# Attention with whole-row loads and one head per TensorE tile, and values @ first matrix as eight tiles, in an attention and two-layer expert kernel

## The chip, the cores and the metric

The kernel runs on one core of one Trainium2 chip. The metric is the time of the program on the device, in microseconds (us), as the median of several executions. TensorE (PE in the profile) multiplies matrices out of SBUF into the banks of PSUM; VectorE (DVE), ScalarE (ACT) and GpSimd (POOL) do elementwise work; SyncE (SP) issues all loads and stores of this kernel, and 16 DMA engines carry them.

## What is computed

Queries, keys and values have 4 batches, 8 heads, 576 rows and 64 columns, and each head has 32 packed rows p. The packed rows attend to the keys and values; then the queries attend to that packed result:

```python
p_packed = sm_attn(p, k, v)               # 32 rows a head
out = sm_attn(q, p_packed, p_packed)      # 576 rows a head
```

`sm_attn` is softmax(scale * Q K^T) V. The result, 2304 tokens by 512 columns, goes through two layers:

```python
h = x @ w_in                              # 512 -> 2048
x = (h * clip(h + 3, 0, 6) / 6) @ w_out   # 2048 -> 512
P = exp(x @ w_gate - max); 8 times: rows, then columns of P normalised
out += P[:, e:e+1] * (relu(x @ w1[e]) @ w2[e])   # for 8 experts, 512 -> 1024 -> 512
```

The two matrices of the first layer come in as 64-bit floats and are taken apart into 32-bit ones on the chip.

## The kernel before, in words

Every large product is made of three passes over operands that are split into a high and a low part (`split_part`, L417 and L422). Small products, those of the attention among them, run on plain float32 operands; such a matmul shows as two passes (two instructions) in the profile.

**Attention** (`attention`, L464) works in eight units of four heads: unit u is batch u // 2 and half u % 2 of its heads. For a unit SP issues four loads of k (L480), p (L489, in the first two units), four loads of q (L497) and one of v (L505). Keys of two heads lie side by side in one tile, so a load of one head writes runs of 64 numbers, 256 bytes, with a gap between them; q likewise. v comes in rows of 6 x 64 numbers, 1,536 bytes. There is one buffer each for k (one per pair of heads), q and v. Then, in this order of dependence:

- 12 transposes of k (L527), three to a bank, each of 96 rows by two heads, and four copies to kT (L293 on ScalarE or L294 on VectorE; this helper makes all copies out of PSUM);
- a transpose of p (L544), and a multiplication with a mask (L549), so that a head's columns stand beside zeros;
- scores of the first attention (L569): four matmuls, 128 rows deep, two heads in 64 columns of TensorE, 288 wide, into two banks; maximum, exponential, sum;
- nine transposes of q (L617), and three copies;
- six transposes of the weights (L637), two copies, and 12 matmuls with v (L653), 96 deep, 64 columns, 128 wide;
- the division, masked (L664, ppz), two transposes (L678) and two copies to ppT, a tile per unit in which each head's packed values stand beside zeros;
- the second scores in two parts, of 384 and 192 columns (L710): 18 matmuls, 128 deep, 64 columns, 64 wide; softmax over each 32 columns; transposes (L768, L772); and copies to a2 in high and low parts.

**First layer.** The result of the second attention is not formed. Instead `packed_weights` (L800) multiplies ppT of a batch's two units with 256 columns of w_in: four matmuls (L810), 128 deep, 64 columns of TensorE, 256 wide, into one bank, eight passes in all. One copy (L825, ScalarE) and one subtraction (L830, VectorE) of 512 columns make the high and low parts pw. `layer1a` (L835) multiplies a2 with pw (L848 to L850), four products of six passes for each of two halves of a batch's rows; ScalarE (L858) and VectorE (L863) apply the activation and with that free the bank. `layer2a` (L870) multiplies with w_out (L885 to L887). The group of `packed_weights` occurs 32 times: four batches by eight groups of 256 hidden units.

The banks of PSUM are shared out by tag: four of `tp` during the attention, and two each of `ph` (pw, layer1a) and `po` (layer2a), which become four each after it (`second_phase`). The group's result and each product of layer1a take one place of `ph`.

**Weights.** `whole` (L386) loads a matrix of a group: for w_in two pieces (`raw_piece`, L375; one DMA each at L381, of 128 partitions by two rows of 2,048 bytes), which `split_f64` takes apart. It has two places, `raw`. The first four groups' weights are loaded during the attention; those of the first two go ahead of unit 0.

**Order.** A planner (`Order`) puts all operations in the order in which each engine takes them: it always picks the operation that can start first by a model of the costs, and among those the most urgent. The costs are written beside each operation. Each engine, SP too, then takes its operations strictly in that order. The routing (L1067 for its product, L1077, L1137) and the eight experts (`layer1b`, L958 to L960; `layer2b`, L1007 to L1009) follow, from about 390 us on.

## Time and profile before

| | |
|---|---|
| three executions | 1982.13, 1979.96, 1975.92 us; median 1979.96 |
| the profiled execution | span 1972.3 us, first to last instruction; no other time of it is given |
| busy, share of the span | TensorE 97%, VectorE 71%, GpSimd 53%, ScalarE 44% |
| granted TensorE clock, mean over the span | 0.996 of full speed |
| DMA | 104.95 MB in 103,553 packets, of which 42,736 are under 512 bytes |
| chain of work that ended last | 71% TensorE's; its largest lines are L1007 to L1009 and L958 to L960 |

The span is that of one execution taken by the profiler. Busy time counts a matmul from its start to its modelled end, and matmuls overlap, so distances between starts are the better measure of what one costs. A group's row gives busy time, mean duration of one and the idle time of its engine just before it, with what ended that. A line of a helper (L293, L417, L422) stands for many operations, so the tile's name matters.

### The profile page before, as it was taken

The page shows a single profiled execution, that of the slowest core. Times are in us where ns is not written, and L with a number is a line of the kernel's source. Part 1 is how long each engine was busy: PE and PEld are TensorE (multiplying, and loading weights), DVE is VectorE, ACT ScalarE, POOL GpSimd, SP SyncE. Part 2 cuts the span into 40 slices and gives each one's busy share as a digit, 9 for nine tenths or more (in the row PEclk, how much of TensorE's full clock was granted, in tenths as well). Part 3 has the DMA queues.
Part 4 walks back from the last instruction along what each step waited for, and adds up shares of the span by engine and source line. Part 5 has one row for each costly group of instructions (what it writes and reads, how often), then busy time and mean ns, then how long its engine had stood idle before and what let it go on. Part 6 is the DMA issues. An engine that isn't in the chain of part 4 may idle for free.

```text
span 1972.3 us, 29636 instructions
## 1 busy us (share of the span) xinstructions
PE 1922.3 (97%) x10957; PEld 1733.2 (88%) x10957; DVE 1392.9 (71%) x2499; ACT 874.1 (44%) x1992; POOL 1052.1 (53%) x1045
## 2 busy tenths in 40 slices
PE   6999999998999999999999999999999999999998
PEld 4789989997888999999889899999999999999997
DVE  6885686437988777777866767667676676767665
ACT  6885775435354444444453334333333333333332
POOL 2454575326787766677744445454454544545442
PEclk9999999999999999999999999999999999999999
DMA  9921121001212221222301111110111111111102
GB/s 212 199 78 33 54 65 44 12 1 32 65 57 67 70 74 66 65 66 74 88 31 43 33 33 34 32 44 33 33 33 33 43 33 33 33 33 43 33 11 65
DMA packets 103553, 104.95 MB, mean 53 GB/s; under 512 B 42736, under 2 KB 78576, under 8 KB 103408
## 3 DMA queue, kind: packets, MB, share of 16 engines
q1 hardware_dynamic: 103408, 103.06, 19.0%
q8 instruction: 86, 1.41, 0.3%
q14 instruction: 59, 0.48, 0.1%
HBM read 98.32 MB, written 4.72 MB: 52 GB/s over the span
## 4 chain that ended last, share of the span: by engine, by line
PE 71%; DVE 4%; issue 1%; ACT 0%; ACTq 0%; DVEq 0%
PE po L1009 13%; PE po L1007 13%; PE po L1008 13%; PE ph L958 11%; PE ph L960 11%; PE ph L959 11%; DVE acc L1025 1%; DVE acc L1019 1%; DVE tmp L936 1%; DVE tmp L967 1%; DVE acc L1031 0%; DVE hsl L422 0%; DVE xyl L422 0%; DVE w1xl L422 0%; ACT tmp L973 0%
## 5 line engine op out<-in xcount | busy, mean ns | idle before, releaser
L422 POOL TENSOR_TENSOR hsl<-tmp,hsh 128x384 fp32r<-128x384 f32 (+1 forms) x503 | 505.1, 1019 | 541.0 <-ACT hsh L417 538.4
L1031 DVE SCALAR_TENSOR_TENSOR acc<-po,Pr,acc 128x512 f32<-128x512 f32 x504 | 373.6, 748 | 186.2 <-PE po L1009 184.8
L967 DVE TENSOR_TENSOR tmp<-ph,tmp 128x384 f32<-128x384 f32 x672 | 364.1, 554 | 165.9 <-PE ph L960 150.3
L1009 PE MATMUL po<-w2h,hsl 128*128 128x512 f32 x1152 | 449.1, 390 | 2.8 <-DVE hsl L422 2.8
L1007 PE MATMUL po<-w2h,hsh 128*128 128x512 f32 x1152 | 449.0, 390 | 1.3 <-ACT hsh L417 1.3
L1008 PE MATMUL po<-w2l,hsh 128*128 128x512 f32 x1152 | 448.8, 390 | 0.0
L973 ACT ACTIVATE tmp<-tmp 128x384 f32<-128x384 f32 x384 | 198.7, 521 | 460.1 <-DVE tmp L967 457.6
L958 PE MATMUL ph<-xyh,w1h 128*128 128x384 f32 x768 | 259.8, 338 | 7.9 <-DVE tmp L967 5.9
L959 PE MATMUL ph<-xyl,w1h 128*128 128x384 f32 x768 | 259.1, 337 | 2.3 <-DVE xyl L422 2.2
L1009 PEld LDWEIGHTS po<-w2h,hsl 128*128 128x128 f32 x1152 | 216.2, 188 | 49.8 <-DVE hsl L422 4.5
L960 PE MATMUL ph<-xyh,w1l 128*128 128x384 f32 x768 | 259.0, 337 | 0.0
L417 ACT ACTIVATE hsh<-tmp 128x384 fp32r<-128x384 f32 (+1 forms) x512 | 245.9, 498 | 22.4 <-DVE tmp L863 10.4
L1007 PEld LDWEIGHTS po<-w2h,hsh 128*128 128x128 f32 x1152 | 216.3, 188 | 43.1 <-ACT hsh L417 1.8
L1008 PEld LDWEIGHTS po<-w2l,hsh 128*128 128x128 f32 x1152 | 216.3, 188 | 41.5
L417 ACT ACTIVATE w2h<-raw 128x1024 fp32r<-128x1024 f32 x64 | 67.9, 1060 | 403.3 <-PE po L1009 394.1
L422 POOL TENSOR_TENSOR w2l<-raw,w2h 128x1024 fp32r<-128x1024 f32 x60 | 145.0, 2416 | 113.6 <-ACT w2h L417 113.6
L958 PE MATMUL ph<-xyh,w1xh 128*128 128x384 f32 x576 | 194.9, 338 | 0.5 <-ACT xyh L417 0.5
L959 PE MATMUL ph<-xyl,w1xh 128*128 128x384 f32 x576 | 194.6, 338 | 0.0
L960 PE MATMUL ph<-xyh,w1xl 128*128 128x384 f32 x576 | 194.4, 338 | 0.0
L958 PEld LDWEIGHTS ph<-xyh,w1h 128*128 128x128 f32 x768 | 144.9, 189 | 14.2 <-DVE tmp L967 4.2
L959 PEld LDWEIGHTS ph<-xyl,w1h 128*128 128x128 f32 x768 | 144.9, 189 | 6.4 <-DVE xyl L422 2.5
L960 PEld LDWEIGHTS ph<-xyh,w1l 128*128 128x128 f32 x768 | 145.0, 189 | 0.0
(186 smaller groups left out, 3242.1 us busy)
## 6 DMA issues: line engine op xcount, KB each, us to landing
raw<-in_moe_w_dram SPq DMA_DIRECT2D x128, 512.0 KB, 3.6
raw<-in_moe_w_in_dram SPq DMA_DIRECT2D x16, 512.0 KB, 3.9
raw<-in_moe_w_out_dram SPq DMA_DIRECT2D x16, 512.0 KB, 3.8
k<-in_k_dram SPq DMA_DIRECT2D x32, 144.0 KB, 5.5
q<-in_q_dram SPq DMA_DIRECT2D x32, 144.0 KB, 4.7
v<-in_v_dram SPq DMA_DIRECT2D x8, 576.0 KB, 6.7
out_dram<-acc SPq DMA_DIRECT2D x36, 128.0 KB, 2.4
p<-in_p_dram SPq DMA_DIRECT2D x1, 224.0 KB, 5.5
```

Source lines behind the costliest of these rows:

```text
L417: t_act(n), lambda: nc.scalar.activation(dst(w.t[0]), src(), AF.Copy),
L422: lambda e: e.tensor_tensor(dst(w.t[1]), src(), as_f32(dst(w.t[0])), ALU.subtract),
L936: lambda e, s=s, i0=i0, i1=i1, how=how: e.tensor_tensor(s.t, i0(), i1(), how),
L958: nc.tensor.matmul(out, wh[:, at + c, :], bh[:, c, :], start=(c == 0), stop=False)
L959: nc.tensor.matmul(out, wh[:, at + c, :], bl[:, c, :], start=False, stop=False)
L960: nc.tensor.matmul(out, wl[:, at + c, :], bh[:, c, :], start=False, stop=(c == 1))
L967: t_dve(n), lambda: nc.vector.tensor_tensor(dst.t, ps.t[:, :n], u.t, ALU.add),
L973: act(t_act(n), lambda: nc.scalar.activation(c.t, c.t, AF.Relu), writes=[c], **quick)
L1007: nc.tensor.matmul(ps.t, hh[:, f, ts], wh[:, f, :], start=(f == 0), stop=False)
L1008: nc.tensor.matmul(ps.t, hh[:, f, ts], wl[:, f, :], start=False, stop=False)
L1009: nc.tensor.matmul(ps.t, hl[:, f, ts], wh[:, f, :], start=False, stop=(f == NFC - 1))
L1031: lambda row=row, share=share, ps=ps: nc.vector.scalar_tensor_tensor(row(), ps.t, share(), row(), ALU.mult, ALU.add),
```

## The change

In the attention, keys are loaded two heads at a time, each head's six rows of a partition as one run of 1,536 bytes, and queries likewise with nine rows, 2,304 bytes: two loads of k and two of q for four of each. The transposes of k and q take two neighbouring rows of one head in place of one row of two heads, so even rows of a head land in the first 64 partitions and odd rows in the other 64. Products then take one head at a time: 64 deep, in TensorE tiles of 64 rows by 32 columns (first scores) or 64 by 64 (second scores, now with 256 and 320 columns), and 96 by 32 for the product with v. Masks, and the memsets that made them, are gone. The transposed packed rows (pt, ppT) hold the same values in both halves of the partitions, in place of values beside zeros.

In the first layer, a group of `packed_weights` is eight matmuls, 64 deep and 32 columns, on eight different tiles of TensorE, for the two units in two banks, with a copy and a subtraction of 256 columns for each bank. w_in is loaded for that in halves of 64 partitions: two DMAs for each piece.

The rest of the diff takes out comments.

```diff
     def raw_piece(src, prio, tag="raw"):
...
+    def raw_halves(srcs, prio, tag="raw"):
+        c, n = srcs[0].shape[1], srcs[0].shape[2]
+        r = hold(tag, [128, c * n], srcs[0].dtype)
+        for h, src in enumerate(srcs):
+            dma(
+                256,
+                lambda h=h, src=src: nc.sync.dma_start(
+                    r.t[64 * h:64 * h + 64].rearrange("p (c n) -> p c n", c=c), src
+                ),
+                fills=[r], prio=prio,
+            )
+        return r
...
         if which == "w1":
-            src = w1[:, f0:f0 + FG].rearrange("(c p) f -> p c f", p=128)
+            halves = [
+                w1[DM // 2 * h:DM // 2 * (h + 1), f0:f0 + FG].rearrange("(c d) f -> d c f", d=D) for h in range(2)
+            ]
+            shape, wide = [128, KC, FG], w1.dtype == I64
+            piece = lambda i, n, tag: raw_halves([s[:, i:i + n, :] for s in halves], prio, tag)
...
-        kp = [tile_of(f"k{g}", [PR, R, 2, D]) for g in range(2)]
+        kp = [tile_of(f"k{g}", [PR, 2, R, D]) for g in range(2)]
...
-        for h in range(4):
+        for g in range(2):
             dma(
                 288,
-                lambda h=h: nc.sync.dma_start(
-                    kp[h // 2].t[:, :, h % 2, :], k[b, 4 * j + h].rearrange("(p r) d -> p r d", r=R)
+                lambda g=g: nc.sync.dma_start(
+                    kp[g].t.rearrange("p h r d -> p h (r d)"),
+                    k[b, 4 * j + 2 * g:4 * j + 2 * g + 2].rearrange("h (p r) d -> p h (r d)", r=R),
                 ),
-                fills=[kp[h // 2]], **kw,
+                writes=[kp[g]], **kw,
             )
...
-                for g in range(2):
+                for h in range(4):
                     nc.tensor.matmul(
-                        s1[a].t[64 * g:64 * g + 64, :HS],
-                        pt.t[:, g, :],
-                        kT.t[:, g, a * HS:(a + 1) * HS],
+                        s1[a].t[32 * h:32 * h + 32, :HS],
+                        pt.t[64 * a:64 * a + 64, 32 * h:32 * h + 32],
+                        kT.t[64 * a:64 * a + 64, 3 * h:3 * h + 3, :].rearrange("p m c -> p (m c)"),
                         start=True, stop=True,
                     )
...
-            for r in range(R):
-                for g in range(2):
+            for n in range(R):
+                a, i = divmod(n, 3)
+                for h in range(4):
                     nc.tensor.matmul(
-                        pp.t[64 * g:64 * g + 64, :128],
-                        a1T.t[:, r, 64 * g:64 * g + 64],
-                        v_sb.t[:, 2 * g:2 * g + 2, r, :],
-                        start=(r == 0), stop=(r == R - 1),
+                        pp.t[32 * h:32 * h + 32, :D],
+                        a1T.t[:, n, 32 * h:32 * h + 32],
+                        v_sb.t[:, h, 2 * i + a, :],
+                        start=(n == 0), stop=(n == R - 1),
                     )
...
+                for h in range(4):
+                    g, o = divmod(h, 2)
+                    for r in range(4):
+                        w, c = r % 2, 128 * (r // 2) + 32 * h
+                        nc.tensor.matmul(
+                            s2.t[64 * w:64 * w + 64, c:c + 32],
+                            qT.t[lo:hi, o, r, 64 * g:64 * g + 64],
+                            ppT.t[lo:hi, 32 * h:32 * h + 32],
+                            start=True, stop=True,
+                        )
...
-        ps, w = psum("ph"), pair("pw", [128, 2, FG])
+        ps, w = [psum("ph") for _ in range(2)], pair("pw", [128, 2, FG])
 
         def mm():
-            for j in range(2):
-                for g in range(2):
+            for c in range(4):
+                for j in range(2):
                     nc.tensor.matmul(
-                        ps.t[64 * g:64 * g + 64, j * FG:(j + 1) * FG],
-                        ppTs[2 * b + j].t[:, g, :],
-                        w1.t[:, 2 * j + g, :],
+                        ps[j].t[32 * c:32 * c + 32, :FG],
+                        ppTs[2 * b + j].t[64 * j:64 * j + 64, 32 * c:32 * c + 32],
+                        w1.t[64 * j:64 * j + 64, c, :],
                         start=True, stop=True,
                     )
...
-                1.0, mm, reads=[ppTs[2 * b], ppTs[2 * b + 1], w1], writes=[ps], takes=[w],
+                0.6, mm, reads=[ppTs[2 * b], ppTs[2 * b + 1], w1], writes=ps, takes=[w],
...
+        for j in range(2):
+            high = act(
+                t_act(FG, True), lambda j=j: nc.scalar.activation(w.t[0][:, j, :], ps[j].t[:, :FG], AF.Copy),
+                reads=[ps[j]], fills=[w], **quick,
+            )
+            dve(
+                t_dve(FG),
+                lambda j=j: nc.vector.tensor_tensor(
+                    w.t[1][:, j, :], ps[j].t[:, :FG], as_f32(w.t[0][:, j, :]), ALU.subtract
+                ),
+                reads=[ps[j]], fills=[w], after=[high], **quick,
+            )
```

## Rows read from the trace of the kernel before

**Rows 1.** The page: span, and TensorE's busy time
```profile
span 1972.3 us, 29636 instructions
...
PE 1922.3 (97%) x10957; PEld 1733.2 (88%) x10957; DVE 1392.9 (71%) x2499; ACT 874.1 (44%) x1992; POOL 1052.1 (53%) x1045
```

**Rows 2.** Stretches (us): length; busy PE, PEld, DVE, ACT, POOL; clock; DMA share; GB/s
```profile
0.00:40.00 40.00, 23.51 (x232) 16.89 (x232) 26.39 (x74) 24.28 (x59) 10.87 (x19) 1.00 1.08 216
40.00:150.00 110.00, 102.03 (x998) 86.15 (x999) 94.87 (x248) 94.21 (x254) 56.23 (x53) 1.00 0.65 141
150.00:450.00 300.00, 295.57 (x2183) 272.88 (x2183) 178.29 (x419) 160.50 (x411) 149.84 (x188) 0.99 0.11 34
```

**Rows 3.** Stretch after 150 us, line 810 alone: length, PE, PEld, clock, DMA
```profile
150.00:470.00 320.00, 26.72 (x192) 11.83 (x192) 0.98 0.11 34
```

**Rows 4.** Timeline of TensorE around a group of line 810: start, us, what
```profile
189.39 0.29 PE L850 MATMUL ph<-a2h,pwl 128*128 128x288 f32 x1
189.62 1.08 PE L810 MATMUL ph<-w1f,ppT 128*64 128x256 f32 x8
190.63 0.40 PE L885 MATMUL po<-hsh,w2h 128*128 128x288 f32 x1
```

**Rows 5.** Timeline of TensorE around the router's product, line 1067
```profile
387.61 0.85 PE L1067 MATMUL ph<-acc,wg 128*32 128x384 f32 x8
388.40 0.40 PE L848 MATMUL ph<-a2h,pwh 128*128 128x288 f32 x1
```

**Rows 6.** Line 1067 within 387.5 to 387.8 us: durations, first and last start
```profile
L1067 PE MATMUL ph<-acc,wg x4: 510/510/511, 387.6 to 387.6; 128*32 128x384 f32 x4
```

**Rows 7.** Timelines: VectorE before the group at 189.62, TensorE around 280.53
```profile
187.95 0.45 DVE L863 SCALAR_TENSOR_TENSOR tmp<-tmp,ph 128x288 f32<-128x288 f32 x1
...
188.76 0.45 DVE L863 SCALAR_TENSOR_TENSOR tmp<-tmp,ph 128x288 f32<-128x288 f32 x1
...
280.53 1.78 PE L810 MATMUL ph<-w1f,ppT 128*64 128x256 f32 x8 [2.21 <-DVE tmp L863]
```

**Rows 8.** Groups by line and shape, whole span: busy us, mean ns, idle before
```profile
L810 PE MATMUL ph<-w1f,ppT 128*64 128x256 f32 x256 | 35.4, 398 | 3.6 <-DVE tmp L863 3.6
...
L830 DVE TENSOR_TENSOR pwl<-ph,pwh 128x512 fp32r<-128x512 f32 x32 | 21.9, 684 | 10.5 <-ACT pwh L825 10.4
...
L825 ACT ACTIVATE pwh<-ph 128x512 fp32r<-128x512 f32 x32 | 18.9, 592 | 1.3 <-PE ph L810 1.3
...
L293 ACT ACTIVATE kT<-tp 128x288 f32<-128x288 f32 x27 | 10.5, 413 | 2.3 <-PE tp L527 2.1
```

**Rows 9.** Groups of TensorE within 0 to 150 us
```profile
L653 PE MATMUL tp<-v,a1T 96*64 96x128 f32 x192 | 12.2, 277 | 0.3 <-ACT a1T L293 0.3
...
L617 PE MATMUL tp<-ident,q 128*128 128x128 f32 x72 | 11.7, 296 | 2.9 <-issue 1.2 <-ACT a L594 1.0 <-DVE e L734 0.6
L569 PE MATMUL tp<-kT,pt 128*64 128x288 f32 x64 | 11.0, 450 | 2.1 <-DVE pt L549 2.1
...
L710 PE MATMUL tp<-ppT,qT 128*64 128x64 f32 x288 | 10.1, 224 | 1.8 <-ACT ppT L293 1.4 <-DVE a2l L783 0.4
```

**Rows 10.** Timeline of TensorE from 0 to 15 us
```profile
7.85 1.19 PE L527 MATMUL tp<-ident,k 96*128 96x96 f32 x6 [7.85 <-DMA k<-in_k_dram]
...
13.95 1.71 PE L569 MATMUL tp<-kT,pt 128*64 128x288 f32 x6 [1.85 <-DVE pt L549]
```

**Rows 11.** Timeline of SP's DMA issues from 0 to 10 us
```profile
0.73 0.94 SPq L381 DMA_DIRECT2D raw<-in_moe_w_in_dram  x2
1.72 3.63 SPq L480 DMA_DIRECT2D k<-in_k_dram  x4
...
8.84 0.73 SPq L505 DMA_DIRECT2D v<-in_v_dram  x1
```

**Rows 12.** The page: DMA issues, KB each, median us to landing
```profile
k<-in_k_dram SPq DMA_DIRECT2D x32, 144.0 KB, 5.5
...
v<-in_v_dram SPq DMA_DIRECT2D x8, 576.0 KB, 6.7
```

More of the change, by code (lines that the diff above doesn't have):

```diff
@@ L346, in split_f64 @@
             t_act(n), lambda: nc.scalar.activation(as_f32(words(1)), as_f32(words(1)), AF.Sign),
-            takes=[r], after=[*r.writers[:1], first], **kw,
+            takes=[r], after=[*r.writers, first], **kw,
         )
@@ L350, in split_f64 @@
             t_act(n), lambda: nc.scalar.activation(as_f32(words(0)), words(0), AF.Copy, scale=2.0 ** -52),
-            takes=[r], after=r.writers[:1], **kw,
+            takes=[r], after=list(r.writers), **kw,
         )
@@ L397, in whole @@
         for i in range(0, shape[1], per):
-            r = raw_piece(src[:, i:i + per, :], prio, turn_of("raw", early))
+            r = piece(i, per, turn_of("raw", early))
             def at(t, i=i, c0=0, n=per * shape[2]):
@@ L461, in tile_kernel @@
     a2 = [pair("a2", [128, 2, S]) for _ in range(B)]
-    ppTs = [hold("ppT", [128, 2, 64]) for _ in range(NU)]
+    ppTs = [hold("ppT", [128, 4 * NP]) for _ in range(NU)]
     def attention(u, p_sb):
@@ L493, in attention @@
             )
[L494 removed]
+        for g in range(2):
             dma(
                 288,
[L497 to L499 removed]
+                lambda g=g: nc.sync.dma_start(
+                    qp.t[64 * g:64 * g + 64].rearrange("p h r d -> p h (r d)"),
+                    q[b, 4 * j + 2 * g:4 * j + 2 * g + 2].rearrange("h (p r) d -> p h (r d)", r=RQ),
                 ),
@@ L674, in attention @@
         ppT = ppTs[u]
-        def trans(ps=ps):
-            for g in range(2):
-                nc.tensor.transpose(ps.t[:, 128 * g:128 * g + 128], ppz.t[:, g, :], ident)
-        pe(0.22, trans, reads=[ppz], writes=[ps], takes=[ppT], **kw)
-        for g in range(2):
-            copy(
-                lambda g=g: ppT.t[:, g, :],
-                lambda g=g, ps=ps: ps.t[:, 128 * g + 64 * g:128 * g + 64 * g + 64],
-                64, reads=[ps], fills=[ppT], **kw,
-            )
-        w = a2[b]
-        for tiles in (range(0, 6), range(6, RQ)):
-            pairs = [t for t in tiles if t % 2 == 0 and t + 1 < RQ]
-            tail = len(tiles) % 2
-            base = 64 * tiles[0]
-            nq = 64 * len(tiles)
+        pe(
+            0.12,
+            lambda ps=ps: nc.tensor.transpose(ps.t[:, :128], ppz.t.rearrange("p a d -> p (a d)"), ident),
+            reads=[ppz], writes=[ps], takes=[ppT], **kw,
+        )
+        copy(lambda: ppT.t, lambda ps=ps: ps.t[:, :128], 128, reads=[ps], fills=[ppT], **kw)
+        w = a2[b]
+        for x in range(2):
+            tail = 1 - x
+            nq = 256 + 64 * tail
             NG = nq // NP
@@ L724, in wide @@
                 return h.t[:, :NG, None].to_broadcast([128, NG, NP])
-            pe(0.15 * len(tiles), scores, reads=[qT, ppT], writes=[s2], takes=[m2, e2, s2s], **kw)
+            pe(0.6, scores, reads=[qT, qL, ppT], writes=[s2], takes=[m2, e2, s2s], **kw)
             dve(
@@ L762, in attention, with trans @@
             ps = bank()
-            n = 128 * len(pairs)
-            def trans(e2v=e2v, ps=ps, pairs=pairs, tail=tail, n=n):
+            def trans(e2v=e2v, ps=ps, tail=tail):
                 flat = e2v().rearrange("p c n -> p (c n)")
-                for i in range(len(pairs)):
+                for i in range(2):
                     nc.tensor.transpose(
```

163 lines of the change are left out of this document (69 added, 94 removed).

## The prediction, made before the changed kernel ran

> **What bounds the kernel now.** I read the page first. TensorE's row says 97% [rows 1], and busy matmuls there are pipelined, so I did not take that for proof; the stretches of the span [rows 2] say where TensorE is not fed. In the first 40 us it is busy for 23.5 us, from 40 to 150 us for 102.0 of 110, from 150 to 450 for 295.6 of 300. So there are three situations: a start in which TensorE waits, a mixed stretch (attention beside the first layer's products) in which all engines are busy, and a long stretch that is TensorE's alone. Work taken off TensorE counts in full in the third, largely in the second, and not in the first; only an earlier arrival of data counts there. The change leaves everything behind the first layer untouched, so all of it must be won before about 470 us.
>
> **values @ matrix (packed_weights), 32 groups of eight passes.** 192 of the 256 passes [rows 8], so 24 groups, run after 150 us [rows 3], the other 8 before it. A regular group stands between the last pass of layer1a at 189.39 and the next product at 190.63 [rows 4]: 1.24 us, where an ordinary pass takes 0.13. From its own start it holds TensorE for 190.63 - 189.62 = 1.01 us. The four matmuls go to two tiles of 64 columns, two at a time; two rounds of two passes would be four slots. What does a slot cost when more tiles are filled? The router's product [rows 5] has four matmuls on four tiles of 32 columns: its eight passes begin at 387.61 and the next product starts at 388.40, 0.79 us later, and four of the eight begin together at 387.6 [rows 6]. If both groups are slots plus one drain, 2 slots of 384 columns + d = 0.79 and 4 slots of 256 + d = 1.01 give (a slot going as its columns) 0.21 us for 256 columns and d = 0.15. That matches: side by side, four tiles cost what one does. Eight matmuls at once would thus take 2 x 0.215 + 0.15 = 0.58 us, plus some 0.05 for sixteen staggered starts: 0.63, a saving of 0.38 to 0.43. But no row shows two tiles that lie under each other, in different halves of the rows; if these take turns the group stays at 4 x 0.215 + 0.15 = 1.01 and saves nothing. The bounds are 0 and 0.43 us; I take 0.40, because the nearest row, the router's, overlaps completely. The Trainium skill, "TensorE: Matmul & The Clock Gate", Part 3 on packing small matmuls, says row tiles overlap as column tiles do, each further tile adding about 4 ns; by it the group would be 0.61 us. No run here shows that yet. 24 groups x 0.40 = 9.6 us count in full, the 8 early ones by half, 1.6: **-11.2 us** (0 to -13).
>
> **Its two banks.** A group now asks for two places of ph instead of one. Directly before a group stand three or four layer1a products, one place each, and there are four places (two during the attention). A place is free when VectorE's L863 has run. Before the group at 189.62 the first two had run by 188.40 and 189.21 [rows 7]: no wait. At 280.53 the group already waited 2.21 us for one place, because L863 was held up behind weight conversion [rows 7]. The second place comes one product later, 0.81 us by the distance of the two L863. I charge 0.2 us to half of the 24 groups: **+2.5 us** (0 to 24 x 0.81 = +19). Behind the waiting matmul stands everything on TensorE, layer2a's products too, unless the planner places these first. The copies get smaller and twice as many: 592 ns on ScalarE and 684 on VectorE per group now [rows 8], and with 256 columns each at least half and at most the 413 ns of 288 columns that kT's copy takes [rows 8]: up to +0.23 us per group on ScalarE, 7 us in all, and as much on VectorE. Both are busy for under 60% from 150 us on [rows 2], so I count 0; without that cover it would be the 7 us.
>
> **Attention's matmuls, eight units.** Busy times of the first 150 us [rows 9], per unit: scores of the first attention L569 11.0/8 = 1.37 us, a1T @ v L653 1.53, second scores L710 1.26, transposes of q L617 1.46. L569: four matmuls of 288 columns on two tiles become eight on eight tiles: from unchanged (row halves take turns) to half of the four 0.24 us slots, -0.5; taken -0.4. L653: twelve matmuls of 128 columns become 24 of 64 on four tiles: six rounds instead of twelve with half the columns each time, from 1.53 to about 0.85; but if a start cannot come quicker than in L710 (18 matmuls in 1.26, less 0.2 of drain, so 0.06 each), 24 x 0.06 = 1.4; taken -0.4. L710: 18 matmuls become 36 with half the columns: 1.26, or 36 x 0.06 + 0.2 = 2.4; taken +0.4. q: ten transposes for nine, +0.16. One transpose of ppz fewer, -0.1. Sum -0.4 per unit, **-3 us** (-9 to +9). Copies: three of kT for four, one of ppT for two, a smaller ppz, together some 0.5 us less per unit on ScalarE and VectorE, which in the mixed stretch are as full as TensorE (94 of 110 us [rows 2]); it is inside the next term's bounds.
>
> **Loads.** The first transposes of keys start at 7.85 us, the first scores at 13.95, having waited for p's path [rows 10]. SP issues four loads of k in 3.63 us, so p goes out at 5.35 at the earliest and v at 8.84 [rows 11]. k moves 144 KB in 5.5 us and v 576 KB, in 1,536-byte rows, in 6.7 [rows 12]: four times the bytes for 1.2 us more. k and q get such rows. Two issues of k at v's 0.73 us instead of four save 2.2 us of SP, two more issues of the first matrix (about 0.47 each by [rows 11]) cost 0.9; then 0.6 MB of keys ahead of p go quicker, about 1 us. I take p and the first scores 2.5 us earlier: **-2.5 us** (0 to -8, half of TensorE's 16.5 idle us before 40). In the mixed stretch TensorE idles 8 us; sooner keys may give back **-1.5** (0 to -5). The doubled loads of the first matrix, 16 more issues in all, wait on SP for places rather than cost time: 0; the eight memsets run while the first keys are on their way: 0.
>
> **Sum.** -11.2 + 2.5 - 3 - 2.5 - 1.5 = -15.7 us. The order is planned anew from other costs, which can shift TensorE's small waits either way; I allow 4 us. The profiled execution spans 1972.3 us, so 1956.6 after. The median of the three runs, 1979.96, is 7.7 above that span (the quickest run is 3.6 above), so the forecast is 1979.96 - 15.7 = **1964 us**.
>
> **Rivals.**
> *Row halves take turns.* No row speaks against it. Then the first term is 0 and L569 gains nothing: -15.7 + 11.2 + 3.2 = about -1, 1979 us: no change. Chance 0.11.
> *The loads hold the whole mixed stretch.* The DMA share is 1.08 up to 40 us and 0.65 to 150 [rows 2], and each unit has one buffer of keys. For it: the median landings [rows 12]. Against: TensorE is busy for 102 of the 110 us all the same, and ScalarE and VectorE nearly as long [rows 2]. Then the two load terms reach their ends, -8 and -5, with the matmul terms as forecast: -24.7, and with the matmuls' own best ends -35: about 1950 us. Chance 0.14.
> *The second bank.* If TensorE loses 0.81 us at each of the 24 later groups, +19 replaces +2.5 and, with the early groups held up by two places likewise (half of them, 8 x 0.81 / 2 = 3), the sum is about +4. With 1.1 us at each, half of the wait at 280.53, it is +11: 1991 us, slower. It decides from about 0.65 us per group on, and beyond what can be measured from 0.9. Against it: all 32 groups hold only 3.6 us of waits now [rows 8] and the planner takes layer2a first when ph is short. The Trainium skill, "TensorEngine Tiling (Array Packing)", Gotcha 1, says two row tiles must not write one bank at the same time and that row tiling raises the pressure on PSUM, which is why the second bank cannot be saved. Chance 0.09.
> *Main forecast*, 0.66.
>
> **How the numbers follow.** About 0.3% (6 us) is what a measurement of this kernel can tell from no change; the three runs differ by that much. The main case lies almost wholly beyond it on the quick side (0.61 of 0.66), the loads' case too: faster 0.61 + 0.14 + 0.01 = 0.76. Same: 0.05 of the main case, 0.09 of the turns: 0.14. Slower: the second bank's 0.09 and 0.01 of the turns: 0.10. The range goes from the loads' rival with a little beyond, 1944, to no change, 1981.
>
> **What the profile will show.** Right if a regular group of eight (sixteen passes) has the next product start about 0.6 us after its first pass instead of 1.01; wrong if it is near 1.0. TensorE's waits for L863 before it should stay under 6 us in all; more means the second bank. L653 busy near 9 us in eight units, L710 near 13. k landing in under 5 us, first scores near 11.5 us. The first layer's end should come some 15 us earlier; if that shift is lost again by 600 us, the routing stretch has eaten it.

## The result, and the profile after the change

The changed kernel takes 1993.35 us (median of four runs, 1989.51 to 1997.7) against 1979.05 for the kernel before beside it. The medians lie 14.3 us apart. The ratio on record is 1.0083, 95% interval [1.0066, 1.0099], or 16.4 us of 1975, and the text goes by it; the record does not say which executions of the kernel before it rests on. So the kernel is some 16 us slower where the forecast had 16 us faster. Its profiled execution took 1989.51 us with a span of 1987.7, 15.4 more than before's [rows 1].

First the stretches of the span, to be held against [rows 2] (columns as there):

```profile
0.00:40.00 40.00, 25.86 (x390) 19.75 (x391) 19.92 (x57) 26.17 (x61) 11.62 (x17) 0.96 0.98 220
40.00:150.00 110.00, 97.19 (x1338) 82.17 (x1337) 89.22 (x236) 84.91 (x225) 38.53 (x39) 0.92 0.51 130
150.00:470.00 320.00, 306.12 (x2513) 279.83 (x2512) 190.70 (x470) 171.12 (x468) 160.39 (x198) 0.99 0.13 36
```

In the mixed stretch all five engines do less (TensorE 97 for 102 us, VectorE 89 for 95, POOL 39 for 56), the transfers too (0.51 for 0.65), and the granted clock is 0.92 for 1.00. Nothing there became the new full engine; the stretch ran thinner, and work slid behind 150 us. When did it slide? The first products of the second matrix (layer2a), first and last start, in the kernel before and in the changed one:

```profile
L885 PE MATMUL po<-hsh,w2h x256: 290/295/609, 77.4 to 452.6; 128*128 128x288 f32 x128
```
```profile
L911 PE MATMUL po<-hsh,w2h x256: 290/295/442, 90.0 to 469.2; 128*128 128x288 f32 x128
```

The first starts 12.6 us later, the last 16.6, and the span ends 15.4 later, so the loss lies in the first 470 us. Where in them, a first start alone does not tell: with another planned order (experiment 6) it comes at 86.4 us instead of 77.4, and no time is lost. A count of finished work tells more. Passes of layer1a and layer2a (L848 to L850 and L885 to L887, and their counterparts) started by 90 us are 78 in the kernel before and 37 in the changed one; by 160 us, 408 and 318; by 450 us, 2276 and 2178. At 0.13 us a pass that is 5, 12 and 13 us: most of the loss arises between 0 and 160 us.

The eight tiles do what they should. A regular group in the changed kernel (timeline, as [rows 4]), one that was held up, and TensorE's waits from 160 to 340 us (total, times, longest):

```profile
170.51 0.66 PE L834 MATMUL ph<-w1f,ppT 64*32 64x256 f32 x16
171.10 0.40 PE L874 MATMUL ph<-a2h,pwh 128*128 128x288 f32 x1
...
260.92 0.62 PE L834 MATMUL ph<-w1f,ppT 64*32 64x256 f32 x2
261.71 0.66 PE L834 MATMUL ph<-w1f,ppT 64*32 64x256 f32 x14 [0.17 <-DVE tmp L889]
262.80 0.40 PE L874 MATMUL ph<-a2h,pwh 128*128 128x288 f32 x1 [0.42 <-DVE tmp L889]
```
```profile
PE ph L834 <- DVE tmp L889: 6.0, 10, 1.4
PE po L912 <- POOL hsl L439: 3.2, 5, 1.5
```

The next product starts 0.59 us after the group's first pass, not 1.01: row halves of the array overlap. But at 260.92 only the first of the eight matmuls (two passes, into the first bank) runs; the second needs a place in the second bank, and it and all behind it start 0.8 us later. The 6.0 us of such waits were 3.3 before, in two waits.

The second scores went the other way. One unit, the changed kernel (lines 716 and 724, 72 passes, the rest left out) and the kernel before:

```profile
35.54 0.42 PE L716 MATMUL tp<-ppT,qT 64*64 64x32 f32 x8 [0.94 <-ACT ppT L291]
...
36.84 0.93 PE L716 MATMUL tp<-ppT,qT 64*64 64x32 f32 x26
37.70 0.71 PE L578 MATMUL tp<-kT,pt 64*32 64x288 f32 x16
```
```profile
36.02 1.25 PE L710 MATMUL tp<-ppT,qT 128*64 128x64 f32 x35
37.10 0.41 PE L569 MATMUL tp<-kT,pt 128*64 128x288 f32 x1
37.11 0.22 PE L710 MATMUL tp<-ppT,qT 128*64 128x64 f32 x1
37.16 0.65 PE L569 MATMUL tp<-kT,pt 128*64 128x288 f32 x3
```

From 35.54 to 37.70 is 2.16 us where some 1.15 stood (36.02 to 37.16). Values times weights gained somewhat more than forecast: line 673 is busy for 7.7 us in the eight units instead of 12.2 [rows 9], where near 9 was expected.

Last the loads: SP's issues from 0 us on, and the page's landings ([rows 11], [rows 12]):

```profile
0.73 2.73 SPq L391 DMA_DIRECT2D raw<-in_moe_w_in_dram  x4
3.51 1.09 SPq L497 DMA_DIRECT2D k<-in_k_dram  x2
4.64 0.45 SPq L507 DMA_DIRECT2D p<-in_p_dram  x1
```
```profile
raw<-in_moe_w_in_dram SPq DMA_DIRECT2D x32, 256.0 KB, 4.3
raw<-in_moe_w_out_dram SPq DMA_DIRECT2D x16, 512.0 KB, 3.6
k<-in_k_dram SPq DMA_DIRECT2D x16, 288.0 KB, 5.9
```

The halves of the first matrix hold SP for 2.73 us where two whole pieces took 0.94, so keys go out 1.8 us later, and a half of 256 KB lands later (4.3 us) than a whole piece of 512 KB did (3.9 in the page of before). A load of keys in whole rows lands no sooner (5.9 for 5.5), though it now carries 288 KB in place of 144.

### The profile page after: what moved, and what is told of

It reads as the page before. It is cut to its first block, busy times and chain, and to the rows that moved or that the text cites. A ratio compares the mean times of both kernels' runs of the same rounds, so it can differ in the third digit from the quotient of the medians.

```text
span 1987.7 us, 31263 instructions
## 1 busy us (share of the span) xinstructions
PE 1926.9 (97%) x11757; PEld 1735.5 (87%) x11757; DVE 1390.1 (70%) x2518; ACT 877.0 (44%) x2020; POOL 1044.6 (53%) x1038
## 4 chain that ended last, share of the span: by engine, by line
PE 71%; DVE 3%; issue 0%; ACT 0%; ACTq 0%; DVEq 0%
PE po L1035 13%; PE po L1033 13%; PE po L1034 13%; PE ph L984 11%; PE ph L986 11%; PE ph L985 11%; DVE tmp L962 1%; DVE tmp L993 0%; DVE acc L1045 0%; DVE acc L1057 0%; DVE hsl L439 0%; DVE acc L1051 0%; DVE xyl L439 0%; ACT tmp L999 0%; DVE w1xl L439 0%
```

## The experiments

Ratios are to the kernel before, run beside each. Where one kernel is set against another of them, the difference of two ratios is uncertain by 0.0014 to 0.0029, 3 to 6 us, if the two half intervals are added in squares.

**1. The second bank.** The kernel before with two banks for a group (product as before), and the changed kernel with its second bank taken from the layer's results:

```diff
-        ps, w = psum("ph"), pair("pw", [128, 2, FG])
+        ps, w = [psum("ph") for _ in range(2)], pair("pw", [128, 2, FG])
...
-        ps, w = [psum("ph") for _ in range(2)], pair("pw", [128, 2, FG])
+        ps, w = [psum("ph"), psum("po")], pair("pw", [128, 2, FG])
```

> The kernel before, its four matmuls of a group as they were, but the two units' results in two places of ph, with a copy and a subtraction of 256 columns each. Theory (the second place is what ate the gain of the eight tiles): groups after 150 us wait again and again for L863, some 0.4 to 0.8 us in a third to half of them, idle before the group's passes up from 3.6 to 10 us or more, and the time is 5 to 12 us above before, 1984 to 1991 us. Rival (the waits come from the newly planned order or the weights' conversion, not from the second place): within 3 us of before.

> The changed kernel with one of a group's two places taken from po, layer2a's tag, in place of a second one from ph. Theory (the second place of ph): the groups between 200 and 330 us lose their 1.0 to 1.9 us from first to last pass and go back to about 0.29, the first layer's stretch is 8 to 11 us shorter, about 1983 us. Rival (waits of the planned order): the waits move to another line, within 3 us of the changed kernel, 1990 to 1996 us.

The first gives 1.0038 [1.0023, 1.0053], 7.5 us lost by the second place together with the doubled copies. The second keeps the doubled copies and gives 1.0043 [1.0027, 1.006] for 1.0083: 7.9 us back. The two agree on the price, so no price of the copies shows. Not as expected, in the first kernel the waits for L863's counterpart before a group behind 150 us do not grow (2.2 us for 3.3). With the other bank part of the waits only moves: between 160 and 340 us TensorE now stands 6.8 us, 13 times, for POOL's hsl (the low parts of the hidden units, which GpSimd makes), where 3.2 stood.

**2. The second scores.** Both query halves interleaved, so that four tiles run instead of two, on the changed kernel and with the other bank:

```diff
-            for h in range(4): ...   # one x at a time
+                    for x in range(2):
+                        nc.tensor.matmul(s2p[x].t[64 * w_:64 * w_ + 64, c:c + 32], ...)
```

> The changed kernel with the two parts of the second scores issued as one piece, passes of the two row halves taking turns, into the same two banks. Theory (a pass with 64 stationary columns holds its tile for some 58 ns however narrow it is, so two tiles at a time gave 30 ns a pass; four tiles give about 15): a unit's 72 passes take 1.1 us in place of 2.15, some 8 to 10 us less of TensorE in the attention, and about 1984 us. Rival (the attention stretch is held by the loads and the chain of each unit, not by TensorE): the passes get quicker, the time stays within 3 us of the changed kernel.

> The changed kernel with both edits: a place of po for a group's second result, and the second scores interleaved. Theory: both gains add up, -16 to -20 us, 1973 to 1977 us, a little quicker than before. Rivals: one of the two is without effect, then about 1983 us; both, then about 1993 us. The granted clock between 20 and 100 us is looked at too: if the half level there comes from the thin passes of the second scores, it is gone or rarer here.

The passes do get quicker. A unit in the interleaved kernel:

```profile
57.88 1.13 PE L711 MATMUL tp<-ppT,qT 64*64 64x32 f32 x64
58.83 0.41 PE L720 MATMUL tp<-ppT,qL 64*64 64x32 f32 x8
59.17 0.53 PE L656 MATMUL tp<-ident,a 128*96 128x128 f32 x3
```

1.29 us instead of 2.16. Yet the times are 1.009 [1.0074, 1.0105] and 1.012 [1.0099, 1.0141]: nothing gained, and with the other bank worse. From 10 to 160 us TensorE is busy for 121.2 us instead of 129.6; what was taken off became idle time, while the granted clock of that stretch went from 0.93 to 0.90. So TensorE's own work alone does not pace that stretch.

**3. Places.** The change also gave pd, pt and ppz one place instead of two, which my prediction overlooked. One place for pd in the kernel before, two in the changed one, two for all three with the other bank, and that with the scores interleaved:

```diff
-        pd = tile_of("pd", [128, 2, D], 2)
+        pd = tile_of("pd", [128, 2, D])
```

> The changed kernel with two places for pd, the tile that GpSimd fills with a unit's packed rows, as the kernel before had (the change left it one). Theory (with one place GpSimd's copy of the next unit waits for TensorE's transpose of this one, 20.9 us in the first 100 us, and the weight conversions of the first groups stand behind it): that wait falls under 6 us, the second w_out of the first pair is ready near 80 us in place of 90.2, the first 96 passes of the first layer end near 100 us in place of 113.7, and the time falls by 6 to 12 us, 1981 to 1987 us. Rival (the conversions are late by the loads of w_in in halves and by the order, GpSimd had time to spare): the wait goes and the time stays within 3 us.

> The kernel before with one place for pd in place of two, nothing else. Theory (the single place holds GpSimd up): GpSimd's wait for the transpose of p rises from 3.1 to 10 us or more in the first 100 us and the time by 4 to 10 us. Rival (the single place matters only with the new order): within 3 us of before.

> The changed kernel with two places each for pd, pt and ppz as before the change, and a group's second result in a place of po. Theory (single places and the second bank are the two causes, apart): both gains add up, -13 to -20 us, 1972 to 1980 us, level with before or a little quicker. Rival (only one of them is real): 1983 to 1987 us.

> As the run with places and po, and the second scores of both row halves issued as one piece. Theory that the second scores cost time once the conversions are on time: a further 4 to 8 us, 1966 to 1974 us. Rival (the attention stretch is still held by the conversions and the chains, not by TensorE): within 3 us of the run with places and po.

Measured 1.008 [1.0065, 1.0095], 1.003 [1.002, 1.0041], 1.0075 [1.0055, 1.0096] and 1.0061 [1.004, 1.0082]. One place costs the kernel before 6 us, but giving it back gains the changed kernel nothing: POOL's waits for it (20.9 us in five up to 100 us) only became 17.5 in three. The third is a miss of its own: with the other bank alone the changed kernel stood at 1.0043, and two places on top of that made it 6.3 us slower. The prices of these side conditions do not simply add up.

**4. The halves of the first matrix.** The kernel before with the changed kernel's halves and all else as it was:

```diff
-            r = raw_piece(src[:, i:i + per, :], prio, turn_of("raw", early))
+            load = raw_halves if which == "w1" else raw_piece
+            r = load(src[:, i:i + per, :], prio, turn_of("raw", early))
```

> The kernel before, with the first layer's first matrices loaded as the changed kernel loads them: each piece in two transfers of 64 partitions and 256 KB; the rows, their places and all of the attention stay as they were. Theory (the conversion of the first groups' weights starts late because the halves land late, and the rest of the mixed stretch is paced by it): the first pieces' waits on a raw piece grow by 2 to 4 us, the first pair's second w_out is ready 4 to 12 us later than 77.5 us, and the time is 1.003 to 1.007 of before. Rival (the lateness comes from the rows of k and q, from the second scores and the second bank, not from the halves): the second w_out within 2 us of 77.5 and a ratio within 1.000 to 1.002.

1.0047 [1.0035, 1.006], 9.3 us. SP's issues in this kernel, and ScalarE's first instructions in the kernel before and in this one, show where the start loses:

```profile
0.74 2.74 SPq L392 DMA_DIRECT2D raw<-in_moe_w_in_dram  x4
3.52 2.79 SPq L494 DMA_DIRECT2D k<-in_k_dram  x4
6.35 1.43 SPq L503 DMA_DIRECT2D p<-in_p_dram  x1
```
```profile
0.73 1.28 ACT L342 ACT_TABLE_LOAD   x1 [0.73 <-PEq L1248]
4.67 0.66 ACT L342 ACTIVATE m_early<-raw 128x512 f32<-128x512 f32 x1 [2.66 <-DMA raw<-in_moe_w_in_dram]
```
```profile
5.81 1.28 ACT L342 ACT_TABLE_LOAD   x1 [5.81 <-DMA raw<-in_moe_w_in_dram]
7.10 0.66 ACT L342 ACTIVATE m_early<-raw 128x512 f32<-128x512 f32 x1
```

Keys go out 1.8 us later and p 1.0 [rows 11]. ScalarE's first conversion of a raw piece begins at 7.10 us instead of 4.67 (7.23 in the changed kernel): the piece is there later, and a table load on ScalarE (ACT_TABLE_LOAD, 1.28 us), which was over before the piece came, now stands behind it. The first product with the second matrix is at 80.3 us, 2.9 late, the last layer2a start at 462.4, 9.8 late; by 160 us 362 passes of layer1a and layer2a have started instead of 408, 6 us at 0.13. What makes the lateness grow on the way is not shown. The Trainium skill, "DMA: Bandwidth & Descriptors", Rules for kernel authors, says two transfers to disjoint halves of the partitions don't help and asks for one over all 128; the trace agrees: 2.74 us of SP's queue for four halves, where two whole pieces take 0.94 [rows 11].

**5. Pieces cut by rows instead.** The same 256 KB transfers, each over all 128 partitions, in the same planned order:

```diff
-                    r.t[64 * h:64 * h + 64].rearrange("p (c n) -> p c n", c=c), src
+                lambda i=i: nc.sync.dma_start(r.t[:, i * n:(i + 1) * n], srcs[:, :, i, :]),
```

> The changed kernel, with the same two transfers of 256 KB for a piece of a first matrix, cut by rows of the contraction instead of by partitions: each writes all 128 partitions. The planned order of every engine is the same, instruction for instruction. Theory A (a transfer into 64 partitions lands late since it is spread over fewer places at its end): the 256 KB transfers land in under 3.5 us by the median instead of 4.3, the first conversions wait 1 to 3 us less, the second w_out is ready 1 to 8 us before 90.2, and the time is 0.996 to 0.999 of the changed kernel's. Theory B (the queue of transfers is what is late, whatever the cut): landing stays 4 to 4.5 us, and the time is the changed kernel's within 0.1 per cent, 1.007 to 1.010 of before.

> The changed kernel with the chunks of the run two before this one, and with the group's second bank in the tag of the layer's results, so that the products' bank has its second place back. If the two faults add up: the second bank gave 0.004 of the time back, the chunks 0.001 to 0.004, so 1.000 to 1.004 of before. If the two meet in the same wait (the planned order that paces the mixed stretch): no better than the second bank's own 1.004.

1.0594 [1.0579, 1.0608] and 1.056 [1.0543, 1.0576]: 117 and 111 us slower, outside both theories. In the first of the two, SP's issues, ScalarE's waits up to 100 us, and the first 50 us (columns as in [rows 2]):

```profile
0.74 10.20 SPq L391 DMA_DIRECT2D raw<-in_moe_w_in_dram  x4
10.97 6.17 SPq L493 DMA_DIRECT2D k<-in_k_dram  x2
```
```profile
ACT m_early L340 <- DMA raw<-in_moe_w_in_dram: 29.3, 3, 11.2
ACT L340 <- DMA raw<-in_moe_w_in_dram: 14.3, 1, 14.3
```
```profile
0.00:50.00 50.00, 10.72 (x127) 7.23 (x129) 9.10 (x23) 14.06 (x30) 4.55 (x12) 0.92 0.32 93
```

The transfers' share is 0.32 at 93 GB/s, where the changed kernel has 0.96 at 221 in the same 50 us. The source of such a transfer is 2 x 64 x 256, its slowest dimension only 2. The same page and section say that a slowest dimension below 16 confines a transfer to as many engines; the rows agree with that, though no run here varied that dimension alone. The first product with the second matrix is at 125.2 us, 48 late, and the last at 571.2, 119 late, with the granted clock at 0.81 from 10 to 160 us. How much of the loss is the loads' own and how much the clock's is not told apart.

**6. The order alone.** The kernel before with one constant of its planner moved:

```diff
-PATIENCE = 0.2
+PATIENCE = 0.25
```

> The kernel before with one constant of its planner moved, PATIENCE from 0.2 to 0.25: no work, no transfer and no place changes, only the order in which the engines take the operations. Theory (the planned order itself is worth several us, and any replanning of the mixed stretch gives some of it away): 1.002 to 1.006 of before, with the loss in the first 390 passes of the first layer. Rival (the order is worth nothing by itself, and the losses of the other experiments come from the things that they changed): within 0.999 to 1.001.

0.9998 [0.9989, 1.0007]. The order changed on every engine, and the time did not: the theory that any new order loses falls. It is one other order only; that the orders planned for the other kernels cost them something is not excluded.

**7. Whole pieces, all eight tiles.** Heads go to the row halves by their parity, so a piece of the first matrix is one transfer again; odd units swap their packed columns in pairs, so that all eight tiles stay distinct. Then the same with the other bank, and with one bank and four tiles (the attention's part alone):

```diff
-                        ps[j].t[32 * c:32 * c + 32, :FG],
-                        ppTs[2 * b + j].t[64 * j:64 * j + 64, 32 * c:32 * c + 32],
-                        w1.t[64 * j:64 * j + 64, c, :],
+                        ps[j].t[32 * (c ^ j):32 * (c ^ j) + 32, :FG],
+                        ppTs[2 * b + j].t[64 * (c % 2):64 * (c % 2) + 64, 32 * c:32 * c + 32],
+                        w1.t[64 * (c % 2):64 * (c % 2) + 64, 2 * j + c // 2, :],
```

> The changed kernel with the first matrices' pieces loaded whole again, in one transfer of 512 KB over 128 partitions, as before. All eight tiles and both banks stay: the heads are given to the row halves by their parity, and the second unit of a batch takes its columns in pairs swapped. Theory (the halves cost the changed kernel what they cost the kernel before, 9 us): 1.003 to 1.005 of before, the second w_out ready 4 to 12 us ahead of 90.2 us. Rival (the lateness is that of the attention itself, and the halves only showed where nothing else was late): 1.007 to 1.010, the second w_out within 3 us of 90.2.

> The run before this one, with the group's second bank in the tag of the layer's results. If halves and bank add up (9 us and 6 us off the changed kernel): 1.000 to 1.002 of before. If the attention in small tiles has a loss of its own under them, or if the two faults hide each other: 1.003 to 1.006. If the saving of the eight tiles comes through once both are gone: 0.996 to 0.999.

> The attention's part of the change alone: whole pieces, one bank for a group's product and one copy and one subtraction of 512 as before; the eight products stand in four tiles, two after the other in each, so a group should take about as long as before (1.0 us). Keys, queries, scores and their tiles are the changed kernel's. Theory (halves and second bank are the whole loss): 0.999 to 1.002 of before. Rival (the attention in small tiles, with 9.8 us more of second scores and 6 us more of transposes, loses 3 us or more of its own): 1.002 to 1.006.

1.0054 [1.0042, 1.0066], 1.0019 [1.0008, 1.003] and 1.0074 [1.0062, 1.0086]. Whole pieces give 5.7 us back, the other bank 6.9 more: undone one at a time in the changed kernel they give 5.7 and 7.9, together 12.6 of the 16.4 us, so these two about add up. The third is a miss: with both gone and only the attention changed, 14.6 us are lost, more than with the eight tiles. The stretch from 10 to 160 us in the last two:

```profile
10.00:160.00 150.00, 131.30 (x1876) 110.15 (x1874) 117.53 (x307) 117.24 (x311) 68.82 (x69) 0.97 0.55 146
```
```profile
10.00:160.00 150.00, 135.12 (x1783) 111.69 (x1782) 110.83 (x286) 114.31 (x291) 55.00 (x54) 0.89 0.56 144
```

The slower one, with the attention alone, has the clock at 0.89, TensorE busier with fewer passes, and its first product with the second matrix at 106.1 us instead of 84.1; by 160 us it has started 312 passes of layer1a and layer2a for 390. A group takes as long in it as before, four tiles and two matmuls on each:

```profile
161.81 1.09 PE L815 MATMUL ph<-w1f,ppT 64*32 64x256 f32 x16
162.82 0.40 PE L890 MATMUL po<-hsh,w2h 128*128 128x288 f32 x1
```

**8. The clock.** TensorE's granted clock has two levels, 2.4 GHz (1.00 in the profile) and 1.2 (0.50). In the changed kernel it stood at the lower one from about 63.0 to 69.6 us, behind eight passes of a unit's first scores and 28 of its 72 passes of second scores. The last 26 passes of a unit's second scores then took 1.58 us, where another unit's took 0.93 (at 36.84, above). The clock of two stretches (columns: length; busy PE; clock; DMA share; GB/s), and the passes at the lower level:

```profile
62.00:63.00 1.00, 1.00 (x30) 1.00 1.11 277
63.00:64.00 1.00, 1.00 (x31) 0.51 0.93 219
```
```profile
63.71 1.58 PE L716 MATMUL tp<-ppT,qT 64*64 64x32 f32 x26
```

Is the lower level the cause? A full product ahead of each of the 16 second scores, in the changed kernel and in the attention alone, should keep it up:

```diff
+                nc.tensor.matmul(
+                    s2.t[:, :256], ident, qT.t[:, 0, 0:2, :].rearrange("p r c -> p (r c)"),
```

> The changed kernel with a full product (128 x 128 stationary, 256 columns, the identity against transposed queries) ahead of each of the 16 second scores, into the same bank, which the scores then write over. The planned order of every engine is unchanged; TensorE has 16 passes and some 7 us more to do. Theory (the new attention loses its time to the clock, which falls while only small tiles run): the granted clock between 10 and 160 us rises from 0.93 to 0.97 or more, and the time is 0.996 to 1.000 of the changed kernel's, 1.003 to 1.008 of before. Rival (the chain of scores and copies paces the stretch): the clock may rise, but the filler's 7 us stand in that chain, and the time is 1.009 to 1.013 of before.

> The kernel with the attention's part of the change alone (whole pieces, one bank, four tiles), with the same filler. Its clock between 10 and 160 us was 0.89, some 34 us at the lower level. Theory (clock): 0.95 or more, and 1.000 to 1.005 of before instead of 1.0074. Rival (chain): 1.008 to 1.012.

1.0119 [1.0101, 1.0136] and 1.0095 [1.0078, 1.0112]: both rivals' ranges. In the order of the text:

```profile
10.00:160.00 150.00, 134.00 (x1733) 107.37 (x1732) 103.85 (x281) 103.82 (x273) 45.69 (x47) 0.89 0.57 141
```
```profile
10.00:160.00 150.00, 133.34 (x1742) 106.02 (x1742) 104.92 (x273) 104.69 (x270) 49.74 (x50) 0.91 0.56 141
```

In these profiled executions the filler hardly moved the clock of the stretch (0.93 to 0.89, 0.89 to 0.91). Over all executions the mean clock of the whole span went from 0.9890 to 0.9905 in the changed kernel and from 0.9874 to 0.9912 in the attention alone. So it could not show what a raised clock would give. It shows that 16 products (32 passes) in the chain of the second scores cost 4 to 7 us, on kernels whose difference is uncertain by 4 to 5.

The record says more about the clock than the filler, because it gives the mean granted clock of every execution. Of the twelve executions of experiment 7's second kernel (whole pieces, other bank), the two at 0.989 took 1983.7 and 1984.5 us, and the three at 0.995 took 1973.6 to 1974.4, level with the kernel before (median 1974.9 beside them); a single one at 0.997 took 1978.7. Of the twelve of experiment 9's kernel, below, the two at 0.993 took 1982.5 and 1983.8 us and the two at 0.997 took 1975.0 and 1976.2. The changed kernel took 1989.5 and 1990.4 at 0.991, 1996.3 and 1997.7 at 0.987. The program is the same each time, so time goes with the clock, by some 1 to 2 us for each 0.001; kernels with four or five executions show it less evenly. The changed kernel's mean is 0.989, that of the kernel before 0.996: by these rows, as an estimate, 7 to 14 of its 16.4 us go with the clock. Whether the lower clock causes them, or late work lowers the clock, no run separates. The kernel before with two banks (mean 0.995) and with halves (0.995) hardly lost any clock, so their 7.5 and 9.3 us are mostly something else. But the changed kernel with the other bank has 0.994, so the 7.9 us that it wins may be in part the clock's.

**9. The eight tiles alone.** The kernel before, loads, scores and attention untouched, with the group's product as eight tiles and the other bank:

```diff
+            for c in range(4):
+                g, o = divmod(c, 2)
+                for j in range(2):
                     nc.tensor.matmul(
-                        ps.t[64 * g:64 * g + 64, j * FG:(j + 1) * FG],
-                        ppTs[2 * b + j].t[:, g, :],
+                        ps[j].t[32 * (c ^ j):32 * (c ^ j) + 32, :FG],
+                        ppTs[2 * b + j].t[64 * o:64 * o + 64, g, 32 * (o ^ j):32 * (o ^ j) + 32],
```

> The kernel before with the group's product as eight tiles at once and nothing else of the change: attention, scores, loads of k, q and of the first matrices stay. The heads are given to the row halves by their parity, the second unit of a batch gets its packed columns in pairs swapped by its own transposes (32 columns each), and the second bank comes from the layer's results. Theory (the eight tiles are worth 10 us wherever the clock and the weights' conversion are in order, as between the attention alone and the run with whole pieces and the other bank): 0.993 to 0.997 of before, with the first 390 passes of the first layer within 3 us of 156.3. Rival (what a product saves becomes a wait for the hidden units' halves and copies, as in the layer's stretch of the changed kernel): 0.998 to 1.003.

1.0018 [1.0009, 1.0026]: the rival. The product's own busy time (line 818, columns as in [rows 3]), TensorE's waits from 150 to 470 us, here and then in the kernel before, and layer2a's products:

```profile
150.00:470.00 320.00, 16.58 (x400) 4.54 (x400) 0.99 0.11 34
```
```profile
PE po L896 <- POOL hsl L422: 6.4, 13, 1.5
PE ph L818 <- DVE tmp L873: 2.9, 3, 1.3
```
```profile
PE ph L810 <- DVE tmp L863: 3.3, 2, 2.2
PE po L886 <- POOL hsl L422: 0.8, 2, 0.5
```
```profile
L895 PE MATMUL po<-hsh,w2h x256: 290/295/402, 84.7 to 454.7; 128*128 128x288 f32 x128
```

Behind 150 us the product holds TensorE 10.1 us less (16.6 for 26.7 [rows 3], and for 25 groups instead of 24). But layer2a waits 6.4 us for POOL's low parts of the hidden units where 0.8 stood, and TensorE's idle time in the stretch rises from 8.8 to 14.7 us. Between the first and the last product with the second matrix lie 370.0 us instead of 375.2. By the count of passes of layer1a and layer2a the kernel is 26 behind at 160 us (382 for 408, 3.4 us at 0.13) and 10 behind at 450 (1.3 us). So 2 to 5 us of the saving are kept there, and a later start takes that and more. What makes the start later in this kernel is not shown. The profiled execution is the quickest of twelve, its span 0.9 us over before's; the ratio stands for 3.6.

## Why the prediction was wrong, step by step

**The eight tiles (-11.2).** The mechanism was right: 0.59 us against a forecast of 0.63. The Trainium skill's figure for packed tiles ("TensorE: Matmul & The Clock Gate", Part 3), by which the prediction had 0.61, is nearer still. The step that failed is "24 groups x 0.40 = 9.6 us count in full". A TensorE busy for 295.6 of 300 us was taken for one that nothing else paces; experiment 9 shows POOL's hsl close behind it (6.4 us of waits for 0.8), and of some 10 us saved 2 to 5 are kept. Alone, with the cheaper bank, the tiles lose 3.6 us; the old product with that bank was not run, so what the tiles lose and what the bank does is not told apart.

**The second bank (+2.5, up to +19).** Mis-sized: 7.5, 7.9 and 6.9 us in three pairs of kernels, and 6.7 between the two of experiment 5. Two pairs say otherwise: with the scores interleaved the other bank loses 6 us (1.009 and 1.012), and with two places it gives back 1 (1.008 and 1.0075), each uncertain by 5. The rival that ended slower had this mechanism, with too small a chance; but not its place: on the kernel before nearly all of the price is paid by 160 us (366 passes of layer1a and layer2a for 408, 5.5 us at 0.13; by 450 us 2231 for 2276, 5.9), where ph has two places and a group takes both, and not at the 24 later groups. Nor does the prediction's "cannot be saved" hold for every split: in experiment 7's third kernel four tiles, two in each row half, write one bank, and a group holds TensorE for 1.01 us: the four slots of the prediction's sum, as tiles that overlap take, and not eight.

**Attention's matmuls (-3).** Second scores were priced at +0.4 per unit and cost +1.0. The start every 0.06 us for a matmul (two passes) that the prediction read from L710 held with half the rows and half the columns (36 matmuls in 2.16 us), so halving the columns saved nothing and twice as many matmuls took twice as long. The prediction had this as its upper bound, 2.4 us, and took a value between. Transposes of q were priced at +0.16 and cost +0.57 (16.3 us busy for 11.7 in eight units). Values times weights gained more than the 0.4 taken (0.56), first scores less (0.29 by busy time, 8.7 us for 11.0). Between experiments 9 and 7 (1.0018 and 1.0019, both with eight tiles, whole pieces and the other bank) lies the whole new attention with its whole-row loads: 0.2 us, nothing beside their uncertainty. Whole rows with the old products were not tried, so the two are not told apart.

**Loads (-4).** The first matrix's doubled loads "wait on SP for places rather than cost time: 0" is the step that failed: 9.3 us alone, 5.7 within the change. They are the first four issues of the queue, ahead of the keys. I counted 0.47 us for each further issue, the trace has 2.73 / 4 = 0.68 for every one, and nothing hid it. Keys did not land in under 5 us. The issue of p came 0.75 us earlier (4.64 for 5.39), but p landed in 7.0 us instead of 5.5, and the first scores began at 12.95 instead of 13.95, not at 11.5.

**The sum** along one path, in us: eight tiles 3.6, new attention and its rows 0.2, second bank in ph 6.9, halves 5.7: the 16.4 measured. As differences of the ratios of neighbouring kernels they add up by construction. It is one path and not a law: the attention on top of the kernel before, with four tiles and one bank, costs 14.6 by itself, and then eight tiles with the other bank take 10.9 of it back. What sets this apart, the clock or the order in which the first weights are converted, stays open; the filler did not settle it. The prediction has no term for the granted clock, which it took as that of the kernel before without a word, and an estimated 7 to 14 us go with it (experiment 8). Nor has it one for the places of pd, pt and ppz: one place for pd costs the kernel before 6 us and the changed one nothing that shows.

**No version of the change beats the kernel before.** The nearest, at 1.0018 and 1.0019, lose 4 us.

## What to carry to other kernels

An engine that is busy for 98% of a stretch is no proof that its work sets the pace: before counting a saving in full, look for the engine that would be late next, and in a planned pipeline suppose that it is a few us behind. A saving on one engine that needs a second buffer, or splits a load at the head of a queue, has to be charged for these at their own measured prices, and those at the start of the queue first. Undo each such side condition by itself on the chip: here a group on eight tiles got quicker as forecast, and undoing its bank and load layout gave most of the loss back. Compare the granted clock of every execution as well as the times, before a loss is put down to a wait.

## What the runs showed of the hardware that was not expected

- Matmuls with a stationary of 64 x 64 and 32 columns start every 0.030 us on two tiles (72 in 2.16 us) and every 0.018 on four (72 in 1.29). Passes of 64 columns on two tiles of 128 x 64 came every 0.032 (36 in 1.15). So a pass of 32 columns costs about what one of 64 does; four tiles at once made it cheaper.
- TensorE's granted clock was 0.81 to 0.97 between 10 and 160 us in every kernel with the new attention and 0.97 to 1.00 with the old one: part of that stretch ran at the 1.2 GHz level. In the changed kernel one such part began at 63.0 us, behind eight passes of first scores and 28 of second scores in small tiles; from 60 to 61 us TensorE had been busy for 0.45 us. A full product ahead of the second scores did not prevent it. Among executions of one program, 0.001 of the span's mean clock went with some 1 to 2 us.
- A transfer of 256 KB whose source has a slowest dimension of 2 held SP for 10.2 us in four issues, and the queue moved 93 GB/s over 50 us, where the same bytes in halves by partition let it move 221.
